# phi(k) of batch 2 issued earlier, k.v of later batches beside mm2 and by 64x64 corners, the z diagonal ahead of phi(q): one change to a linear-attention plus SwiGLU kernel

## The chip, the cores and the metric

The kernel runs on one core of a Trainium2 chip. The metric is the device time of one execution in microseconds; medians of several executions are quoted. The granted TensorE clock of each execution is recorded too.

The engines are called as in the profile: PE (TensorE, matmuls), PEld (its weight loads), DVE (VectorE), ACT (ScalarE), POOL (GpSimd), SP (the DMA queue used for outputs and transposes).

## The reference, cut to what matters

Linear attention over 8 batches (8 heads, 576 tokens, head dimension 64), then a SwiGLU block with 512 inputs, 1536 hidden, 512 outputs, on all 4608 tokens:

```python
q_p, k_p = phi(q), phi(k)                     # phi(x) = elu(x) + 1
kv  = einsum('bhsd,bhse->bhde', k_p, v)       # 64x64 per head
z   = sum(k_p, axis=2)
num = einsum('bhsd,bhde->bhse', q_p, kv)
den = einsum('bhsd,bhd->bhs', q_p, z)[..., None] + 1e-6
x   = (num / den) as (4608, 512)
out = (silu(x @ w_gate) * (x @ w_val)) @ w_out
```

## The kernel before: the parts that the change and the argument touch

The tokens go through the block in nine groups of 512. Each group is L1 (12 blocks of 4 + 4 matmuls 128x512, for gate and value) and then L2 (4 blocks of 12 matmuls). The attention of later batches is woven in: while group g is in L1 and L2, batch g+1 (`b1`) is prepared and mm2 makes the next `xT`, and exp and phi of batch g+2 (`b2`) run in L2. Lists of closures per slot say what is issued behind which block.

Names used below: `pG`, `pV` and `pX` are PSUM banks, which hold results of matmuls; to evict a bank is to copy its result out, so that it can be written again. `osb` holds results of L2 on their way out, `xT` is the input of L1, `R` the copy of k.v that mm2 multiplies by, `zd` the diagonal matrix from which one matmul ("the z matmul") makes z for the denominators, and s3 the steps that divide q by them. In the views `64*128` is the part of the array that a matmul uses (rows * columns), and `64x129` is the operand that streams through it, here 129 columns (N=129). An excursion is a stretch of matmuls in 64-row tiles between matmuls on the whole array.

```python
    def mm1(b, lp):                                  # k.v; lp = pair of heads
        if lp == 0:
            kvb[b] = (bank(), bank()) if b > 1 else ...
        W = 2 * D + (b > 1)                          # 129: v of two heads and a column of ones
        for j in range(J):                           # J = 9
            for (t, term_) in enumerate(terms_k(b, lp)):
                for hh in range(2):                  # rows 0..63 and 64..127 of the array
                    ...
                    nc.tensor.matmul(
                        out=kvb[b][hh][:, 256 * lp:256 * lp + W], lhsT=term_[rows, j, P * lp:P * lp + P], rhs=vv, ...)

    def zdiag(b, lp):                                # DVE: diagonal of z from the column of ones
        for hh in range(2):
            nc.vector.tensor_scalar(out=zd[:, 2 * hh + lp, :], in0=id16[:, :],
                                    scalar1=kvb[b][hh][:, 256 * lp + D:256 * lp + D + 1], ...)

    def steady(b, late=0):                           # what is woven into L1, by slot
        sl = [[] for _ in range(late)] + at(FB, [
            (0, lambda: phi_q(b, 0)), (1, lambda: phi_q(b, 1)), (1, lambda: mm1(b, 0)), (1, lambda: mm1(b, 1)),
            (2, lambda: zdiag(b, 0)), (2, lambda: zdiag(b, 1)), (2, lambda: r_copies(b)),
            (3 + (late > 0), lambda: zb(b)), ...     # zb: one matmul, ones x zd
    ...
    def first():                                     # woven into L1 and L2 of group 0
        ...
            (3, lambda: den1(0)), (4, lambda: num1(0)), (5, lambda: den1(1)), (6, lambda: num1(1)),
            (7, lambda: den2()), (7, lambda: exp_k(2, 0)), (7, lambda: exp_k(2, 1)), (8, lambda: num2()),
            (8, lambda: phi_k(2, 0)), (9, lambda: phi_k(2, 1)), (10, lambda: exp_q(2, 0)), (11, lambda: exp_q(2, 1))])
    ...
        for t in range(4):                           # L2 of group g
            if t == 3 and b1 < NG:
                mm2(b1, pV[2], "AVAV")               # 64x64 corners: num of the next group
            ...
            l2(g, t)
            ...
            l2_out(g, t, A if t == 1 else V)         # evict pso to osb, store
```

Of a product k.v over two heads (128 x 128) only the two 64x64 blocks on the diagonal are used; the old form computes all four.

## Time and profile before

| | before |
|---|---|
| median of 4 runs | 329.74 us (328.22 to 331.26) |
| profiled execution, span | 327.7 us |
| PE busy | 317.2 us (97%) |
| DVE, ACT busy | 216.2, 167.8 us (66%, 51%) |
| one 128x512 matmul, from start to the next start | 216 ns |

The busy time of PE is not its work: matmul records overlap (a 128x512 matmul is recorded with 380 ns, yet the next one starts after 216 ns). So I count by the start times in the timeline.

The page's first two parts, its busy times and the two lines of PE (busy tenths per slice; granted clock per slice in tenths):

```profile
PE 317.2 (97%) x1975; PEld 150.1 (46%) x1975; DVE 216.2 (66%) x400; ACT 167.8 (51%) x239; POOL 31.5 (10%) x47
PE   8999996899999999999999999999999999999994
PEclk9999999799999999999999999999999999999999
```

One dent, at 55 to 62 us: first idle, then a lower clock. The waits view of PE (who waited for whom: us in total, times, longest):

```profile
PE pG L280 <- DVE osb L311: 3.7, 1, 3.7
...
```

The windows view around it (busy us of each engine, then the granted clock, the DMA share, GB/s):

```profile
54.60:58.40 3.80, 0.12 (x1) 0.00 (x0) 3.77 (x8) 3.78 (x4) 0.10 (x1) 0.99 1.21 207
58.40:61.80 3.40, 3.37 (x9) 1.16 (x9) 1.17 (x2) 1.99 (x3) 0.64 (x1) 0.51 1.19 240
```

PE stands still for 3.8 us and then works 3.4 us at clock 0.51. What DVE does meanwhile is in its timeline (start, us, line, operation, count, idle before and who ended it):

```profile
53.42 0.46 DVE L125 TENSOR_SCALAR ek<-ek 128x1152 f16<-128x1152 f16 x1 [0.17 <-ACT ek L121]
53.91 1.43 DVE L127 SCALAR_TENSOR_TENSOR kp<-k,ek 128x576 f16<-128x576 f16 x2
55.26 0.68 DVE L311 TENSOR_SCALAR osb<-pV 128x512 f32<-128x512 f32 x1
55.86 0.45 DVE L125 TENSOR_SCALAR ek<-ek 128x1152 f16<-128x1152 f16 x1
56.34 1.43 DVE L127 SCALAR_TENSOR_TENSOR kp<-k,ek 128x576 f16<-128x576 f16 x2
57.69 0.68 DVE L311 TENSOR_SCALAR osb<-pG 128x512 f32<-128x512 f32 x1
```

The bank `pG` that L1 of group 1 needs first is evicted at 57.69, behind both halves of phi(k) of batch 2.

In the later groups k.v stands inside L1. The timeline of PE in group 2:

```profile
95.72 1.03 PE L280 MATMUL pV<-xT,wv 128*128 128x512 f16 x4
96.68 1.20 PE L170 MATMUL pX<-vm,kp 64*128 64x129 f16 x36
97.81 1.04 PE L280 MATMUL pG<-xT,wg 128*128 128x512 f16 x4
...
100.41 1.03 PE L280 MATMUL pV<-xT,wv 128*128 128x512 f16 x4
101.44 0.38 PE L200 MATMUL pX<-zd,ones 128*128 128x512 f16 x1
```

Four L1 matmuls take 0.863 us, so k.v could have started at 96.58: 0.10 us are lost in front of it. It holds PE from 96.68 to 97.81, 1.13 us.

### The profile page before, as it was taken

The page shows a single profiled execution, that of the slowest core. Times are in us where ns is not written, and L with a number is a line of the kernel's source. Part 1 is how long each engine was busy: PE and PEld are TensorE (multiplying, and loading weights), DVE is VectorE, ACT ScalarE, POOL GpSimd, SP SyncE. Part 2 cuts the span into 40 slices and gives each one's busy share as a digit, 9 for nine tenths or more (in the row PEclk, how much of TensorE's full clock was granted, in tenths as well). Part 3 has the DMA queues.
Part 4 walks back from the last instruction along what each step waited for, and adds up shares of the span by engine and source line. Part 5 has one row for each costly group of instructions (what it writes and reads, how often), then busy time and mean ns, then how long its engine had stood idle before and what let it go on. Part 6 is the DMA issues. An engine that isn't in the chain of part 4 may idle for free.

```text
span 327.7 us, 5115 instructions
## 1 busy us (share of the span) xinstructions
PE 317.2 (97%) x1975; PEld 150.1 (46%) x1975; DVE 216.2 (66%) x400; ACT 167.8 (51%) x239; POOL 31.5 (10%) x47
## 2 busy tenths in 40 slices
PE   8999996899999999999999999999999999999994
PEld 6644452344444444444444445444444444444443
DVE  3757747489978886889588858885887344234321
ACT  2869969536744584468446844584431233123310
POOL 8545300010001000100010000000000000000000
PEclk9999999799999999999999999999999999999999
DMA  7999999958386448553846440134012410140014
GB/s 102 195 200 200 205 207 208 249 98 157 79 169 92 79 89 162 78 92 80 169 65 107 67 112 0 26 71 95 14 24 50 98 30 2 33 92 4 2 32 96
DMA packets 40984, 32.18 MB, mean 98 GB/s; under 512 B 16256, under 2 KB 36480, under 8 KB 40960
## 3 DMA queue, kind: packets, MB, share of 16 engines
q0 software_dynamic: 20640, 18.88, 37.1%
q1 hardware_dynamic: 20160, 12.85, 17.7%
q8 instruction: 15, 0.25, 0.3%
q10 hardware_dynamic: 160, 0.13, 0.2%
q14 instruction: 9, 0.07, 0.1%
HBM read 37.75 MB, written 9.44 MB: 144 GB/s over the span
## 4 chain that ended last, share of the span: by engine, by line
PE 90%; DVE 4%; DMA 3%; ACT 1%; issue 1%; POOL 1%; SPq 0%; POOLq 0%; DVEq 0%; ACTq 0%
PE pV L280 27%; PE pG L280 27%; PE pV L301 14%; PE pG L301 13%; PE pX L280 2%; DMA q<-in_q_dram 2%; PE pX L170 2%; PE pX L252 2%; DVE kp L127 1%; DVE qp L127 1%; DMA out_dram<-osb 1%; PE pX L200 1%; DVE osb L311 1%; DVE hT L286 0%; ACT eq L367 0%
## 5 line engine op out<-in xcount | busy, mean ns | idle before, releaser
L280 PE MATMUL pG<-xT,wg 128*128 128x512 f16 x408 | 105.9, 382 | 3.7 <-DVE osb L311 3.7
L280 PE MATMUL pV<-xT,wv 128*128 128x512 f16 x420 | 108.9, 381 | 0.0
L285 ACT ACTIVATE sil<-pG 128x512 f16<-128x512 f32 x102 | 60.6, 598 | 92.6 <-PE pG L280 83.7
L286 DVE SCALAR_TENSOR_TENSOR hT<-pV,sil 128x512 f16<-128x512 f32 x105 | 72.2, 690 | 52.6 <-PE pV L280 40.0
L280 PEld LDWEIGHTS <-wg 128*128 128x128 f16 x432 | 41.5, 98 | 54.9 <-issue 6.8
L280 PEld LDWEIGHTS <-wv 128*128 128x128 f16 x432 | 42.4, 98 | 51.8 <-issue 1.1
L301 PEld LDWEIGHTS <-hT 128*128 128x128 f16 x420 | 39.8, 98 | 48.4 <-issue 2.0
L301 PE MATMUL pV<-wo,hT 128*128 128x512 f16 x216 | 50.2, 379 | 0.0
L301 PE MATMUL pG<-wo,hT 128*128 128x512 f16 x204 | 47.6, 380 | 0.0
L311 DVE TENSOR_SCALAR osb<-pV 128x512 f32<-128x512 f32 x18 | 12.4, 689 | 22.9 <-PE pV L301 22.9
L127 DVE SCALAR_TENSOR_TENSOR kp<-k,ek 128x576 f16<-128x576 f16 x24 | 17.1, 755 | 0.4
L127 DVE SCALAR_TENSOR_TENSOR qp<-q,eq 128x576 f16<-128x576 f16 x24 | 17.1, 755 | 0.4
L233 DVE TENSOR_TENSOR qp<-qp,rden 128x768 f16<-128x768 f16 x18 | 17.1, 951 | 0.2
L220 DVE TENSOR_REDUCE den<-prod 128x12 f32<-128x768 f16 x18 | 17.0, 942 | 0.0
L267 ACT ACTIVATE xT<-pX 128x512 f16<-128x512 f32 (+1 forms) x14 | 7.4, 579 | 16.7 <-PE pX L252 9.3
L121 ACT ACTIVATE ek<-k 128x1152 f16<-128x1152 f16 x14 | 15.5, 1154 | 0.1
L121 ACT ACTIVATE eq<-q 128x1152 f16<-128x1152 f16 x14 | 15.4, 1148 | 0.0
L147 ACT ACTIVATE vm<-v 128x1152 f16<-128x1152 f16 x12 | 14.1, 1172 | 0.0
L309 ACT ACTIVATE osb<-pG 128x512 f32<-128x512 f32 x8 | 4.7, 583 | 16.3 <-PE pG L301 16.3
L96 POOL DMA_DIRECT2D k<-in_k_dram x7 | 5.2, 742 | 76.4 <-DVE kp L127 54.9
L311 DVE TENSOR_SCALAR osb<-pG 128x512 f32<-128x512 f32 x9 | 6.2, 689 | 9.4 <-PE pG L301 9.4
L363 PE MATMUL pX<-sil,ones 128*128 128x256 f16 x51 | 8.9, 349 | 1.3 <-DVE sil L354 1.3
(97 smaller groups left out, 225.1 us busy)
## 6 DMA issues: line engine op xcount, KB each, us to landing
out_dram<-osb SPq DMA_DIRECT2D x70, 128.0 KB, 2.4
k<-in_k_dram POOLq DMA_DIRECT2D x7, 576.0 KB, 11.6
q<-in_q_dram POOLq DMA_DIRECT2D x7, 576.0 KB, 6.1
v<-in_v_dram POOLq DMA_DIRECT2D x7, 576.0 KB, 8.7
wg<-in_moe_w_gate_dram POOLq DMA_DIRECT2D x6, 256.0 KB, 12.1
wv<-in_moe_w_val_dram POOLq DMA_DIRECT2D x6, 256.0 KB, 12.0
wo<-in_moe_w_out_dram POOLq DMA_DIRECT2D x3, 512.0 KB, 15.8
k<-in_k_dram POOLq DMA_DIRECT2D x2, 288.0 KB, 5.9
```

Source lines behind the costliest of these rows:

```text
L121: nc.scalar.activation(out=e[:, s, :], in_=src[b % 2][:, s, :], func=AF.Exp, bias=0.0, scale=1.0)
L127: nc.vector.scalar_tensor_tensor(out=dst[b % 2][:, :, D * l:D * l + D], in0=src[b % 2][:, l, :].rearrange("p (j d) -> p j d", d=D), scalar ...
L147: nc.scalar.activation(out=vm[b % 2][:, :, s, 0:D].rearrange("p j l d -> p l j d"), in_=v16[b % 2][:, s, :].rearrange("p l (j d) -> p l j ...
L220: nc.vector.tensor_reduce(out=den[:, HL * j0:HL * j1], in_=prod[:, 0:j1 - j0, :].rearrange("p j (l d) -> p (j l) d", d=D), axis=AX.X, op=A ...
L233: nc.vector.tensor_tensor(out=qv, in0=qv, in1=rden[:, HL * j0:HL * j1].unsqueeze(2).to_broadcast([P, HL * (j1 - j0), D]), op=ALU.mult)
L267: nc.scalar.activation(out=dst, in_=ps[i][:, c00:], func=AF.Copy, bias=0.0, scale=1.0 / SC)
L280: nc.tensor.matmul(out=ps[:, :], lhsT=src[:, i, P * fb:P * fb + P], rhs=xT[i][g % 2][:, :], start=(i == 0), stop=(i == 3))
L285: nc.scalar.activation(out=s[:, :], in_=pg[:, :], func=AF.Silu, bias=0.0, scale=1.0)
L286: nc.vector.scalar_tensor_tensor(out=hT[g % 2][:, fb, :], in0=pv[:, :], scalar=SC, in1=s[:, :], op0=ALU.mult, op1=ALU.mult)
L301: nc.tensor.matmul(out=pso[(g, t)][:, :], lhsT=hT[g % 2][:, fb, P * t:P * t + P], rhs=wo[:, fb, :], start=(fb == 0), stop=(fb == FB - 1))
L311: nc.vector.tensor_scalar(out=o[:, :], in0=ps[:, :], scalar1=1.0 / SC, scalar2=None, op0=ALU.mult)
L363: nc.tensor.matmul(out=dst[:, 0:256], lhsT=ones[:, :], rhs=sil[0][:, 0:256], start=True, stop=True)
```

## The change

Its intent: at the boundary of groups 0 and 1, do phi(k) of batch 2 earlier so that the evictions are not behind it; move k.v of batches 3 to 7 next to mm2 in L2, where the array is in 64-row tiles anyway, using two banks that L2 has finished with; build the z diagonal before phi(q) on DVE; compute only the two useful 64x64 blocks of k.v.

```diff
 def mm1(b, lp):
-            kvb[b] = (bank(), bank()) if b > 1 else ((pV[2], pX[0]), (pX[2], pV[2]))[b]
+            kvb[b] = ((pV[2], pX[0]), (pX[2], pV[2]), (pX[0], pX[1]), (pV[0], pG[0]))[min(b, 3)]
...                                                  # batches 0 and 1 stay as they were; else:
+                    for e in range(2):
+                        nc.tensor.matmul(
+                            out=kvb[b][hh][D * e:D * e + D, 256 * lp:256 * lp + D + 1],
+                            lhsT=term_[rows, j, P * lp + D * e:P * lp + D * e + D],
+                            rhs=vm[b % 2][rows, j, 2 * lp + e, :], start=(j == 0), stop=(j == J - 1))
...
 def first():
-            (3, den1(0)), (4, num1(0)), (5, den1(1)), (6, num1(1)),
-            (7, den2()), (7, exp_k(2, 0)), (7, exp_k(2, 1)), (8, num2()),
-            (8, phi_k(2, 0)), (9, phi_k(2, 1)), (10, exp_q(2, 0)), (11, exp_q(2, 1))])
+            (3, den1(0)), (4, num1(0)), (4, exp_k(2, 0)), (5, den1(1)),
+            (5, phi_k(2, 0)), (6, num1(1)), (6, exp_k(2, 1)), (7, den2()),
+            (9, phi_k(2, 1)), (10, num2()), (10, exp_q(2, 0)), (11, exp_q(2, 1))])
...
+    def joint(b):                                   # k.v, z diagonal, R copies
+        for lp in range(2): mm1(b, lp)
+        for lp in range(2): zdiag(b, lp)
+        r_copies(b)
...
 def steady(b):                                       # batch 2: vcast, phi_q, joint in slots 0 to 3 of L1, z in slot 5
-            (0, phi_q(b, 0)), (1, phi_q(b, 1)), (1, mm1(b, 0)), (1, mm1(b, 1)), (2, zdiag ...), (2, r_copies(b)), (3, zb(b)) ...
+            (0, phi_q(b, 1)), (2, zb(b)) ...         # batches 3 on
 def prep(b):
+                      (3, preload of the silu table), (3, phi_q(b, 0))
...
             if t == 3 and b1 < NG:
                 mm2(b1, pV[2], "AVAV")
+                if b2 < B:
+                    joint(b2)
...
-            l2_out(g, t, A if t == 1 else V)
+            l2_out(g, t, A if t in (1, 3) else V)
```

(Lambdas are left out in the diff. The cast of v of batch 2 moved from the boundary into L1 of group 1, and in L2 what is left of s3 is now issued ahead of exp and phi of the batch after.)

More of the change, by code (lines that the diff above doesn't have):

```diff
@@ L67 @@
     epst = sb.tile([P, 1], FP32, name="epst")
-    R = two([P, 4, P + 1], FP16, "R")
+    R = two([P, 4, P], FP16, "R")
     qT = two([P, J, 2, P], FP16, "qT")
@@ L159, in mm1 @@
         if lp == 0:
-            kvb[b] = (bank(), bank()) if b > 1 else ((pV[2], pX[0]), (pX[2], pV[2]))[b]
-        W = 2 * D + (b > 1)
+            kvb[b] = ((pV[2], pX[0]), (pX[2], pV[2]), (pX[0], pX[1]), (pV[0], pG[0]))[min(b, 3)]
         for j in range(J):
@@ L166, in mm1 @@
                     if b < 2:
-                        vv = v16[b][rows, 2 * lp:2 * lp + 2, D * j:D * j + D]
-                    else:
-                        vv = vm[b % 2][rows, j, :, :].rearrange("p l c -> p (l c)")[:, 130 * lp:130 * lp + W]
-                    nc.tensor.matmul(
-                        out=kvb[b][hh][:, 256 * lp:256 * lp + W], lhsT=term_[rows, j, P * lp:P * lp + P], rhs=vv,
-                        start=(j == 0 and t == 0), stop=(j == J - 1 and t == len(terms_k(b, lp)) - 1))
+                        nc.tensor.matmul(
+                            out=kvb[b][hh][:, 256 * lp:256 * lp + P], lhsT=term_[rows, j, P * lp:P * lp + P],
+                            rhs=v16[b][rows, 2 * lp:2 * lp + 2, D * j:D * j + D],
+                            start=(j == 0 and t == 0), stop=(j == J - 1 and t == len(terms_k(b, lp)) - 1))
+                        continue
+                    for e in range(2):
+                        nc.tensor.matmul(
+                            out=kvb[b][hh][D * e:D * e + D, 256 * lp:256 * lp + D + 1],
+                            lhsT=term_[rows, j, P * lp + D * e:P * lp + D * e + D],
+                            rhs=vm[b % 2][rows, j, 2 * lp + e, :], start=(j == 0), stop=(j == J - 1))
     def zdiag(b, lp):
@@ L180, in r_copies @@
     def r_copies(b):
-        W = 2 * D + (b > 1)
+        W = D
         for hh in range(2):
@@ L188, in kv @@
     def kv(b):
-        c1 = D + (b > 1)
+        c1 = D if b < 2 else 0
         return lambda i, e: R[b % 2][D * e:D * e + D, i, c1 * e:c1 * e + D]
@@ L569, in first @@
             (2, lambda: t1(pX[0], 7, 9, A)), (2, lambda: mm1(1, 0)), (2, lambda: mm1(1, 1)), (2, lambda: r1_copies()),
-            (3, lambda: den1(0)), (4, lambda: num1(0)), (5, lambda: den1(1)), (6, lambda: num1(1)),
-            (7, lambda: den2()), (7, lambda: exp_k(2, 0)), (7, lambda: exp_k(2, 1)), (8, lambda: num2()),
-            (8, lambda: phi_k(2, 0)), (9, lambda: phi_k(2, 1)), (10, lambda: exp_q(2, 0)), (11, lambda: exp_q(2, 1))])
+            (3, lambda: den1(0)), (4, lambda: num1(0)), (4, lambda: exp_k(2, 0)), (5, lambda: den1(1)),
@@ L573, in first @@
+            (5, lambda: phi_k(2, 0)), (6, lambda: num1(1)), (6, lambda: exp_k(2, 1)), (7, lambda: den2()),
+            (9, lambda: phi_k(2, 1)), (10, lambda: num2()), (10, lambda: exp_q(2, 0)), (11, lambda: exp_q(2, 1))])
         return sl, w
-    def steady(b, late=0):
-        sl = [[] for _ in range(late)] + at(FB, [
-            (0, lambda: phi_q(b, 0)), (1, lambda: phi_q(b, 1)), (1, lambda: mm1(b, 0)), (1, lambda: mm1(b, 1)),
-            (2, lambda: zdiag(b, 0)), (2, lambda: zdiag(b, 1)), (2, lambda: r_copies(b)),
-            (3 + (late > 0), lambda: zb(b)), (3 + (late > 0), lambda: zb_copy(b)), (3 + (late > 0), lambda: s3_prod(b, 0)),
-            (4, lambda: s3_reduce(b, 0)), (5, lambda: s3_recip(b, 0)), (5, lambda: s3_prod(b, 1)),
-            (6, lambda: s3_scale(b, 0)), (7, lambda: s3_reduce(b, 1)), (7, lambda: tr(b, 0)),
-            (8, lambda: s3_recip(b, 1)), (8, lambda: s3_prod(b, 2)), (9, lambda: s3_scale(b, 1)),
-            (10, lambda: s3_reduce(b, 2)), (10, lambda: tr(b, 1)), (11, lambda: s3_recip(b, 2))])
-        w = at(4, [(0, f) for f in sum(sl[FB:], [])] + [(0, lambda: s3_scale(b, 2)), (0, lambda: tr(b, 2))])
-        if b == 2:
-            sl[0] += [lambda: vcast(2, 1)]
-        return sl[:FB], w
@@ new lines, in joint, with steady @@
+    def joint(b):
+        for lp in range(2):
+            mm1(b, lp)
+        for lp in range(2):
+            zdiag(b, lp)
+        r_copies(b)
+    def steady(b):
+        n = 5 if b == 2 else 2
+        items = [(n, lambda: zb(b)), (n, lambda: zb_copy(b)), (n, lambda: s3_prod(b, 0)),
+                 (n + 1, lambda: s3_reduce(b, 0)), (n + 2, lambda: s3_recip(b, 0)), (n + 2, lambda: s3_prod(b, 1)),
+                 (n + 3, lambda: s3_scale(b, 0)), (n + 4, lambda: s3_reduce(b, 1)), (n + 4, lambda: tr(b, 0)),
+                 (n + 5, lambda: s3_recip(b, 1)), (n + 5, lambda: s3_prod(b, 2)), (n + 6, lambda: s3_scale(b, 1)),
+                 (n + 7, lambda: s3_reduce(b, 2)), (n + 7, lambda: tr(b, 1)), (n + 8, lambda: s3_recip(b, 2)),
+                 (n + 9, lambda: s3_scale(b, 2)), (n + 9, lambda: tr(b, 2))]
+        if b == 2:
+            items = [(0, lambda: vcast(2, 0)), (1, lambda: vcast(2, 1)), (1, lambda: phi_q(2, 0)),
+                     (2, lambda: phi_q(2, 1)), (3, lambda: joint(2))] + items
+        else:
+            items = [(0, lambda: phi_q(b, 1))] + items
+        return at(FB, [x for x in items if x[0] < FB]), at(4, [(0, f) for (i, f) in items if i >= FB])
@@ L590, in prep @@
     def prep(b):
         return at(4, [(0, lambda: exp_k(b, 0)), (0, lambda: exp_k(b, 1)), (1, lambda: exp_q(b, 0)),
-                      (1, lambda: exp_q(b, 1)), (1, lambda: phi_k(b, 0)), (2, lambda: phi_k(b, 1))])
+                      (1, lambda: exp_q(b, 1)), (1, lambda: phi_k(b, 0)), (2, lambda: phi_k(b, 1)),
+                      (3, lambda: nc.scalar.preload_act_table_set("silu_and_others")), (3, lambda: phi_q(b, 0))])
     def ld_b(b):
@@ L640 @@
                 l2_out(0, t, V)
-    vcast(2, 0)
     nc.scalar.preload_act_table_set("silu_and_others")
@@ L648 @@
         if b1 < B:
-            sl, w = steady(b1, 2 if g == 1 else 0)
+            sl, w = steady(b1)
         if b2 < B:
@@ L668 @@
             l2(g, t)
-            for f in pre[t]:
+            for f in w[t] + pre[t]:
                 f()
-            for f in w[t]:
-                f()
-            l2_out(g, t, A if t == 1 else V)
+            l2_out(g, t, A if t in (1, 3) else V)
 _INS = ['q', 'k', 'v', 'moe_w_gate', 'moe_w_val', 'moe_w_out']
```

## The prediction

> **What bounds it now.** TensorE. The page has PE busy 317.2 of 327.7 us, but matmul records overlap, so I count from start to start in the timeline: 128x512 matmuls follow each other every 216 ns. The waits view shows one large wait of PE: 3.7 us at 54.7 us, L1 of group 1 on the DVE eviction of `osb`. After it the windows view gives half clock (0.51) from 58.4 to 61.8 us; the next 32 matmuls take 8.62 us instead of 6.91. The Trainium skill, "TensorE: Matmul & The Clock Gate" (the HAM clock gate), says that an idle window of about 3.4 us halves the clock; this trace agrees. The boundary costs 5.6 us together.
>
> In each later group k.v (36 matmuls 64*128, N=129) takes 1.13 us inside L1, with 0.10 us lost before it and 0.13 to 0.32 us in the 16 L1 matmuls after it: about 1.4 us. mm2 (8 or 16 matmuls 64*64) takes 0.45 to 0.57 us in L2.
>
> **What the change does.**
> 1. Boundary of groups 0 and 1. DVE now does phi(k) of batch 2 where it waited for `rr` (2.7 us), and the `num2` products move behind the second eviction. Adding up trace durations (exp 1.15, ln 0.6, `rr` exp 0.95, phi(k) 1.9 per half, eviction 0.68, x products 0.6 us): exp(k) at 47.9 and 51.1, second phi(k) 52.9 to 54.8, eviction of `pG` done at 55.4 instead of 58.4. L2 ends at 54.6: an idle of 0.9 us is left, and 0.3 us before the second L1 block, too short to halve the clock. K of batch 2 lands at 46.95 us, in time. Saved: 2.7 us of wait, 1.7 us of clock, 4.4 together.
> 2. k.v of batches 3 to 7 beside mm2: one excursion to 64-row tiles fewer. The skill, "TensorEngine Tiling (Array Packing)", Key Properties, says a change of mode drains TensorE; the 0.10 us before k.v agrees. Corners make 72 matmuls of N=65 from 36 of 129. In mm2 a set of four 64*64 matmuls costs its N columns plus about 27 ns (80 ns at N=128, 187 at N=384). 18 sets of about 54 ns are 1.0 us: the corners themselves save little. Saved: 1.4 - 1.0 = 0.4 us, 2.1 in five groups. Batch 2 keeps its own excursion: nothing.
> 3. Banks `pV[0]` and `pG[0]`: DVE evicts `osb` and two `xT`, builds z (0.8 us), then ACT copies R (0.7 us). Added up, R is copied 3.4 us after mm2 starts; the next L1 starts 4.1 us after it. It fits by 0.6 us. phi(k) ends about 1.2 us before k.v.
> 4. phi(q) and s3 earlier: DVE only, off the critical path.
>
> **Time.** 4.4 + 2.1 = 6.5 us, nearly all critical: 2.0%. I take off 0.4 us for small new waits: 323.5 us, 8 in 10 between 321.3 and 326.5. Faster by over 2%: 0.42; within 2%: 0.56; slower: 0.02.
>
> **What would show it.** Right: the wait on `osb` is near 1 us and no slice is at half clock; k.v follows mm2 at once, 72 matmuls in 0.9 to 1.1 us; no wait of PE on R or zd. Wrong: a wait on `osb` over 2 us; k.v over 1.3 us; L1 waiting for R at each group's start.
>
> **What would make it wrong.** If small matmuls start no faster than about 25 ns each whatever their tile, k.v by corners takes 1.8 us and loses 0.4 us in each group. If DVE is later than added up, the L2 banks come free too late. If the clock still drops, 1.7 us stay.

## The result, and the profile after

After: 320.8 us median of 4 runs (320.79 to 320.97), before 329.74; ratio 0.973, 95% interval 0.9685 to 0.9775: faster, and below the low end of my range (321.3). A ratio here is the mean time of one kernel's runs over that of the other's of the same rounds, so not quite the ratio of the medians.

The same lines of the page:

```profile
PE 311.8 (98%) x2191; PEld 148.5 (47%) x2191; DVE 211.3 (66%) x393; ACT 171.3 (54%) x246; POOL 31.9 (10%) x47
PE   8999999999999999999999999999999999999994
PEclk9999999999999999999999999999999999999999
```

The dent is gone. The waits view and the windows view:

```profile
...
PE pG L282 <- DVE osb L313: 0.6, 1, 0.6
...
```

```profile
52.00:55.50 3.50, 3.01 (x21) 1.15 (x20) 3.47 (x7) 3.47 (x6) 0.04 (x1) 1.00 1.22 209
55.50:58.90 3.40, 3.21 (x15) 1.39 (x15) 2.71 (x8) 3.37 (x5) 0.70 (x1) 1.00 1.18 239
```

And DVE at the boundary:

```profile
49.82 1.43 DVE L127 SCALAR_TENSOR_TENSOR kp<-k,ek 128x576 f16<-128x576 f16 x2
...
52.42 0.68 DVE L313 TENSOR_SCALAR osb<-pV 128x512 f32<-128x512 f32 x1
53.02 0.45 DVE L125 TENSOR_SCALAR ek<-ek 128x1152 f16<-128x1152 f16 x1
53.50 1.43 DVE L127 SCALAR_TENSOR_TENSOR kp<-k,ek 128x576 f16<-128x576 f16 x2
54.85 0.68 DVE L313 TENSOR_SCALAR osb<-pG 128x512 f32<-128x512 f32 x1
```

`pG` is evicted at 55.53; I had added up 55.4. The boundary did what was predicted. The timeline of PE in the L2 of group 2, where mm2 and k.v now stand together (first and last lines):

```profile
117.95 0.35 PE L254 MATMUL pX<-qT,R 64*64 64x192 f16 x5
...
118.41 0.19 PE L172 MATMUL pV<-vm,kp 64*64 64x65 f16 x1
...
119.02 0.20 PE L172 MATMUL pG<-vm,kp 64*64 64x65 f16 x2
119.15 2.76 PE L303 MATMUL pG<-wo,hT 128*128 128x512 f16 x12
```

k.v holds PE from 118.41 to 119.15, 0.74 us, not the 1.0 that I had predicted. No wait of PE on R or `zd` appears in its waits view.

Where the 8.5 us of the profiled spans (327.7 to 319.2) went, by the start of the first matmul of each stage:

| stage | before, us | after, us | difference |
|---|---|---|---|
| start to L2 of group 0 | 38.83 | 39.09 | +0.26 |
| L2 of group 0, to the first L1 matmul of group 1 | 19.60 | 16.50 | -3.10 |
| first 32 L1 matmuls of group 1 (clock) | 8.62 | 7.26 | -1.36 |
| k.v of batch 2, in L1 of group 1 | 1.13 | 0.71 | -0.42 |
| rest of L1 of group 1 | 14.04 | 14.04 | 0.00 |
| L2 of group 1 (now with k.v of batch 3) | 10.92 | 11.56 | +0.64 |
| groups 2 to 6 | 166.89 | 162.41 | -4.48 |
| groups 7 and 8 | 67.66 | 67.64 | -0.02 |

The boundary gives 3.10 + 1.36 = 4.5 us (predicted 4.4). Batches 3 to 7 give 4.48 - 0.64 = 3.8 us (predicted 2.1), batch 2 gives 0.4 us (predicted nothing).

### The profile page after: what moved, and what is told of

Its sections match the earlier page's. It is cut to its first block, busy times and chain, and to the rows that moved or that the text cites. A ratio compares the mean times of both kernels' runs of the same rounds, so it can differ in the third digit from the quotient of the medians.

```text
span 319.2 us, 5573 instructions
## 1 busy us (share of the span) xinstructions
PE 311.8 (98%) x2191; PEld 148.5 (47%) x2191; DVE 211.3 (66%) x393; ACT 171.3 (54%) x246; POOL 31.9 (10%) x47
## 4 chain that ended last, share of the span: by engine, by line
PE 89%; DMA 4%; DVE 2%; POOL 2%; ACT 2%; issue 1%; SPq 0%; POOLq 0%; ACTq 0%
PE pV L282 28%; PE pG L282 27%; PE pV L303 14%; PE pG L303 13%; DMA wv<-in_moe_w_val_dram 3%; PE pX L282 2%; PE pX L254 1%; DVE osb L313 1%; DMA out_dram<-osb 1%; PE pV L172 1%; DVE xT L435 1%; ACT rr L432 1%; ACT rr L429 1%; POOL k L99 0%; POOL v L99 0%
## 5 line engine op out<-in xcount | busy, mean ns | idle before, releaser
L311 ACT ACTIVATE osb<-pG 128x512 f32<-128x512 f32 x15 | 8.8, 589 | 19.9 <-PE pG L303 19.8
L217 DVE TENSOR_TENSOR prod<-qp,zbc 128x768 f16<-128x768 f16 x18 | 9.3, 516 | 1.4 <-ACT zbc L208 1.3
```

Source lines behind the costliest of these rows:

```text
L217: nc.vector.tensor_tensor(out=prod[:, 0:j1 - j0, :], in0=qp[b % 2][:, j0:j1, :], in1=zbc[:, :].unsqueeze(1).to_broadcast([P, j1 - j0, HL * ...
```

## The experiments

Three parts were changed together: the boundary, the place of k.v (with the DVE order around it), and the corners. My miss lies in the last two. The theories: A, a set of four corners takes its columns plus a few ns, wherever it stands; B, corners are as dear as I had predicted (54 ns per set) and the place beside mm2 did the rest; later C, the rate at which matmuls start sets the time of a set, not its columns.

### The kernel before with corners alone

```diff
 mm1, batches 2 to 7: one matmul 64*128 of 129 columns
-> two matmuls 64*64 of 65 columns (as in the change), at the old place in L1; R copies and kv() to match
```

> The kernel before with k.v of batches 2 to 7 by 64x64 corners, at its old place inside L1; nothing else. Theory A (corners are cheap wherever they stand: weights of one set load behind the columns of the set before, 33 ns per set of four at N=65): k.v takes 0.71 to 0.75 us instead of 1.13, six times 0.4 us, so about 327.3 us against 329.7 (ratio 0.993), gap and half clock at the boundary as before. Rival B (my prediction: 54 ns per set; corners gain only where they stand directly behind mm2): k.v 1.0 to 1.1 us here, ratio 0.998 to 1.0.

Measured: 329.25 us, ratio 0.9988 (0.995 to 1.0027), same. By the time alone B would seem right. The trace says otherwise; group 2, PE and then DVE:

```profile
96.37 0.78 PE L172 MATMUL pX<-vm,kp 64*64 64x65 f16 x72
97.08 1.04 PE L282 MATMUL pG<-xT,wg 128*128 128x512 f16 x4
...
99.68 1.03 PE L282 MATMUL pV<-xT,wv 128*128 128x512 f16 x4
101.14 0.38 PE L202 MATMUL pX<-zd,ones 128*128 128x512 f16 x1 [0.43 <-DVE zd L179]
```

```profile
97.86 0.45 DVE L125 TENSOR_SCALAR eq<-eq 128x1152 f16<-128x1152 f16 x1
98.35 1.43 DVE L127 SCALAR_TENSOR_TENSOR qp<-q,eq 128x576 f16<-128x576 f16 x2
99.69 0.68 DVE L288 SCALAR_TENSOR_TENSOR hT<-pV,sil 128x512 f16<-128x512 f32 x1
100.29 0.80 DVE L179 TENSOR_SCALAR zd<-id,pX 128x128 f16<-128x128 f16 x4
```

The corners did take 0.71 us instead of 1.13, in all six batches. But the z matmul then waits for `zd`, which stands behind phi(q) in DVE's queue and comes no earlier. The 0.42 us are given back as a wait in five groups (the waits view sums it to 2.0 us); only batch 2 keeps its gain. Theory A is right on the cost, and my expectation from it was wrong on the time.

### The same, with the z diagonal ahead of phi(q)

```diff
-            (0, phi_q(b, 0)), (1, phi_q(b, 1)), (1, mm1(b, 0)), (1, mm1(b, 1)), (2, zdiag(b, 0)), (2, zdiag(b, 1)), (2, r_copies(b)),
+            (0, mm1(b, 0)), (0, mm1(b, 1)), (1, zdiag(b, 0)), (1, zdiag(b, 1)), (1, r_copies(b)), (1, phi_q(b, 0)), (2, phi_q(b, 1)),
```

> The kernel before with corners at the old place in L1, and the z diagonal put ahead of phi(q) on VectorE with k.v one slot earlier. In the run with corners alone the z matmul waited 0.4 us for zd in five groups and ate the gain. If the order on VectorE is the cause: no wait on zd, 2.0 us (and the 0.17 us per group that the kernel before lost there) less than that run: about 326.8 us against 329.3. If the wait has another cause: still 329 us.

Measured: 326.57 us, ratio 0.9899 (0.9853 to 0.9946); no wait of PE on `zd` is left. DVE in group 2:

```profile
97.10 0.75 DVE L179 TENSOR_SCALAR zd<-id,pX 128x128 f16<-128x128 f16 x4
97.76 0.45 DVE L125 TENSOR_SCALAR eq<-eq 128x1152 f16<-128x1152 f16 x1
98.25 1.43 DVE L127 SCALAR_TENSOR_TENSOR qp<-q,eq 128x576 f16<-128x576 f16 x2
```

The times hold the clock of the boundary too: two of the four executions had a granted clock of 1.00 (325.80 and 325.97 us), two had less (327.16 and 328.02). Against the executions of the kernel before at the same clock in these rounds they are on average 2.5 to 3.1 us faster.

The order on DVE was the cause of the wait. This run also put k.v one slot earlier, but the run with k.v back in L1 below tells the two apart: there k.v and the z matmul stand where they stand with corners alone, only phi(q) is done earlier, and no wait on `zd` is left either. Corners make PE earlier, the order lets it use that. The order without corners was not run; from the trace of before it could give no more than the 0.12 to 0.31 us a group that the z matmul was late there.

### The change with the old form of k.v at the new place

```diff
 the kernel after, but mm1 of batches 2 to 7 as before: 36 matmuls 64*128, N=129
```

> The kernel after, with k.v of batches 2 to 7 in the old form (36 matmuls 64*128, N=129), at its new place. Theory A: k.v takes 1.0 to 1.15 us instead of 0.74, six times 0.3 to 0.4 us, so about 322.9 us (ratio to before 0.979). Rival B (the place alone did it): as after, 320.8 us (0.973).

Measured: 323.62 us, ratio 0.9816 (0.9773 to 0.986); k.v takes 1.13 us beside mm2 as it did in L1. Corners are worth 2.8 us of the change (323.62 to 320.8), not the little that I had predicted. Rival B falls. It is 0.7 us slower than theory A expected; most of that is mm2's exit, which k.v in 64*128 tiles does not save (in group 2 mm2 holds PE for 0.56 us here and 0.46 in the kernel after; 0.10 us in each of five groups).

### The change with k.v back in L1

```diff
-        n = 5 if b == 2 else 2
+        n = 5 if b == 2 else 3
-            items = [(0, phi_q(b, 1))] + items
+            items = [(0, phi_q(b, 1)), (1, mm1(b, 0)), (1, mm1(b, 1)), (2, zdiag(b, 0)), (2, zdiag(b, 1)), (2, r_copies(b))] + items
-                if b2 < B:
-                    joint(b2)
 and k.v of batches 3 to 7 in two banks of pX again
```

> The kernel after, with k.v, z diagonal and R copies of batches 3 to 7 put back into L1 (k.v in slot 1, z matmul in slot 3), corners and the early phi(q) of the first half kept. Value of the place alone: its own drain and mode change cost 0.10 us before and 0.10 us after k.v in five groups, 1.0 us: 321.8 us (ratio to before 0.976). If the z matmul then waits for zd as in the run with corners alone (0.4 us five times): up to 323.8 us.

Measured: 321.67 us, ratio 0.9748 (0.9705 to 0.9792), no wait on `zd`. The place itself is worth 0.18 us a group by the traces (table below), 0.8 to 0.9 us in all; the first theory of the expectation holds. (This run and the kernel after were timed in different rounds, so the traces are the better measure.)

The runs line up when only group 2 is measured, from its first L1 matmul to that of group 3, which the boundary does not touch:

| kernel | group 2, us |
|---|---|
| before | 33.36 |
| corners alone | 33.37 |
| corners, z diagonal first | 32.78 |
| after, k.v back in L1 | 32.78 |
| after, old form of k.v | 33.09 |
| after | 32.60 |

Groups 3 to 5 agree with this within 0.05 us, but for one: with corners and z diagonal first they take 32.87 us, because k.v takes 0.80 us there instead of 0.71 (not followed further).

### How long a set of four corners takes

I had taken 27 ns per set on top of the columns. Two looks, each with the same 72 matmuls per batch and other widths:

```diff
-   out=kvb[b][hh][D * e:D * e + D, 256 * lp:256 * lp + D + 1],      rhs=vm[b % 2][rows, j, 2 * lp + e, :]
+   out=kvb[b][hh][D * e:D * e + D, 256 * lp + 32:256 * lp + D + 1], rhs=vm[b % 2][rows, j, 2 * lp + e, 32:]     # N=33
+   out=kvb[b][hh][D * e:D * e + D, 256 * lp:256 * lp + 2 * D + 1],  rhs=both heads of vm, 129 columns           # N=129
```

> The kernel after, corners of k.v with 33 columns (values 32 to 63 and the ones) instead of 65; wrong results on purpose, same number of instructions. Theory A (a set of four takes its columns, N/2.4 ns, plus about 6 ns): 20 ns per set, k.v beside mm2 0.50 us instead of 0.74. Rival C (matmuls of this kind start about 8 ns apart whatever N is; the start times in the trace are 8.3 ns apart in the second half): stays at 0.72 to 0.75 us.

> The kernel after, corners of k.v with 129 columns instead of 65 (each corner multiplies both heads of the pair, as the old form did), correct results, same number of instructions, twice the columns. Theory A: 60 ns per set, k.v 1.15 to 1.25 us, so by itself as slow as the old form (1.13 us). Rival C: between, columns and starts overlap: 54 ns per set, 1.05 to 1.15 us. If my prediction's 27 ns per set were right at all: 81 ns, 1.5 us or more.

One execution each: 321.01 us for N=33 (wrong results) and 323.42 us for N=129 (correct). The timelines of PE at k.v of batch 2, N=33 and then N=129:

```profile
62.98 0.75 PE L172 MATMUL pX<-vm,kp 64*64 64x33 f16 x72
63.66 1.04 PE L282 MATMUL pG<-xT,wg 128*128 128x512 f16 x4
```

```profile
62.95 1.22 PE L172 MATMUL pX<-vm,kp 64*64 64x129 f16 x72
64.10 1.04 PE L282 MATMUL pG<-xT,wg 128*128 128x512 f16 x4
```

To the next L1 matmul that is 0.69 us at N=33, 0.71 at N=65 (in the kernel after) and 1.15 at N=129. From the start times inside k.v beside mm2, a set of four takes 33 to 34 ns at N=33, the same at N=65, and 57 ns at N=129 (means within each half of the 18 sets; between the halves two sets take 50 and 53 ns at N=33 and at N=65, which stays unexplained). Halving the columns from 65 shortens k.v by only 0.02 to 0.03 us, so theory A's form (columns plus 6 ns) falls and C holds: about 8.3 ns from one matmul to the next is the limit below some 80 columns (an estimate: 33 ns x 2.4 columns per ns, from 216 ns for 512), the columns above it. What sets the 8.3 ns stays open: every one of these matmuls also loads its own weights, and no run separates the start of a matmul from the load or from the supply of instructions. At N=129 the corners take as long as the 36 old matmuls (1.13 us beside mm2 for both). So the gain inside k.v is in the columns that are no longer computed, 129 to 65, as far as that limit allows; more and smaller tiles for the same columns save nothing there, only mm2's exit (group 2 takes 32.99 us with corners of N=129 and 33.09 with the old form).

### The boundary alone, and the clock alone

```diff
 the kernel before with the new slots of first(), and vcast(2, 0), vcast(2, 1) in slots 0 and 1 of L1 of group 1
```

> The kernel before with only the reordered work at the boundary of groups 0 and 1 (exp and phi of k of batch 2 between the den and num steps, num2 later, cast of v into L1). If the boundary is worth what I predicted: wait on osb about 0.8 us instead of 3.7, no half clock, 4.4 us less, about 325.3 us (ratio 0.9865). If part of that was given back in L1 of group 1 (DVE late there): 2 to 3 us less, with the first matmuls of L1 over 216 ns apart.

Measured: 325.33 us, ratio 0.987 (0.9834 to 0.9907). The waits view of PE:

```profile
...
PE pG L280 <- DVE osb L311: 0.6, 1, 0.6
...
```

The profiled span is 4.5 us shorter (327.7 to 323.2), as predicted, and no half clock comes before the last 2.2 us; the medians differ by 4.9 us. That the time itself was met to 0.03 us is luck: the kernel before was 0.5 us slower in these rounds than in the first. The first 32 L1 matmuls of group 1 take 7.26 us here, 0.35 more than at 216 ns each (the prediction had 0.3 us there); behind them nothing was given back.

```diff
+    warm(30, pX[0])            # dummy matmuls, 256 columns, results unused
     for g in range(1, NG):
```

> The kernel before with 30 dummy matmuls of 256 columns (about 3.2 us, results unused) put on TensorE where it idles 3.7 us before group 1; the wait on osb itself stays. If the half clock comes from that idle: the next 32 matmuls take 6.9 us instead of 8.6, 1.7 us less in the profile, about 328.0 us (ratio 0.995), and the scatter of before's times (3 us) shrinks to a few tenths. If the half clock has another cause: it stays, ratio 1.0.

Measured: 328.72 us, ratio 0.997 (0.9931 to 1.0008): by the time alone, not told from before. The windows view of this run, behind the gap:

```profile
59.40:66.40 7.00, 6.98 (x32) 3.03 (x31) 4.04 (x7) 3.98 (x6) 0.64 (x1) 1.00 1.17 255
```

L1 still starts 3.9 us after L2 ends, yet its first 32 matmuls take 7.00 us at full clock instead of 8.62 at half. The idle is the cause of the half clock. (The scatter of this run is 0.9 us, not the few tenths that were expected.) Why the median gains only about 1.5 us (330.21 in these rounds): before does not lose the clock every time. Of its seven executions here, the two with a granted clock of 1.00 took 328.28 and 328.66 us, the two at 0.987 took 330.88 and 331.51, three at 0.991 to 0.992 lie between. The four with the gap filled lie at 0.996 to 1.00 and within 328.27 to 329.16 us; no execution of the kernel after is below 0.996 (in its profiled one the half clock comes only in the last 1.3 us, when the work is over). So most of the scatter of before is the clock.

That the same idle does not always cost the clock can be seen in a trace. The run with corners and z diagonal first has the boundary of before, and PE stands still for 3.7 us; its windows view in the gap and behind it shows full clock:

```profile
55.60:59.20 3.60, 0.00 (x0) 0.00 (x0) 3.57 (x7) 3.58 (x4) 0.04 (x1) 1.00 1.21 207
59.30:66.20 6.90, 6.90 (x101) 3.37 (x101) 3.20 (x5) 3.34 (x5) 0.60 (x1) 1.00 1.17 256
```

### Can it be beaten?

0.6 us of waiting at the boundary and 0.35 us in the first L1 blocks are left in the kernel after. Two versions were run next to it; on that chip the kernel after was timed again:

> The kernel after again, on the chip of the next two runs, to compare them with: 320.8 us, ratio to before 0.973.

Measured: 321.13 us, ratio 0.9746 (0.9724 to 0.9768).

```diff
-            (9, phi_k(2, 1)), (10, num2()) ...
+            (10, num2()) ...
                 l2_out(0, t, V)
+    phi_k(2, 1)                 # behind the four evictions of group 0
```

> The kernel after, with phi(k) of the second half of batch 2 behind the four evictions of group 0 instead of ahead of the second one. L1 of group 1 waits 0.75 us for the eviction of pG and 0.35 us more inside its first 32 matmuls; with the eviction directly behind L2's second block both waits go: 1.0 us less, 319.8 us. If DVE is then late in L1 of group 1 (phi(k), two phi(q), z), the gain comes back as waits there: 320.8 us.

Measured: 320.23 us, ratio 0.9718 (0.9694 to 0.9742). L1 of group 1 starts without a wait and its first 32 matmuls take 7.00 us. Some comes back: the z matmul of batch 2 starts 0.13 us late and the L1 matmul behind it another 0.27 us late. DVE, which now does phi(k) here, is the likely reason; the trace was not followed further.

```diff
+ as the run before, and mm1 of batches 0 and 1 by corners of 64 columns
```

> As the run before, and k.v of batches 0 and 1 by corners as well (54 matmul pairs in the start, 18 in L2 of group 0, N=64). Where TensorE is the limit a pair of N=128 takes 55 ns and a set of four N=64 about 33: batch 1 gains 0.4 us; batch 0 at most 1.2 us if TensorE is the limit there, nothing if it waits for loads and DVE. 318.8 to 319.5 us.

Measured: 321.07 us, ratio 0.9744 (0.9718 to 0.977), and a wider scatter (319.93 to 322.5): a miss. Batch 1 did go from 1.11 to 0.71 us. But in the start, PE stops for 1.8 us in the middle of batch 0's corners, with no releaser in the trace:

```profile
16.03 0.20 PE L166 MATMUL pV<-v,kp 64*64 64x64 f16 x2
18.00 0.22 PE L166 MATMUL pX<-v,kp 64*64 64x64 f16 x2 [1.76 <-issue]
```

"Issue" means that the profile shows nothing that it waited for. A transfer of 16 KB on the queue called "instruction" lies at 15.5 to 16.5 us in that trace, while the loads keep the DMA engines full, so a late supply of instructions is a guess; it was not tested. (The kernel after has such a transfer at 15.2 to 16.2 us without a stop, so the transfer alone is not enough.)

```diff
+ phi_k(2, 1) behind the evictions; k.v of batch 1 alone by corners; zb(2), zb_copy(2), s3_prod(2, 0) one slot later
```

> The kernel after with three edits: phi(k) of the second half of batch 2 behind the evictions (as in the run before: 320.2 us), k.v of batch 1 by corners (0.71 instead of 1.11 us in the run with all corners), and the z matmul of batch 2 one slot later, where it waited 0.3 us for zd after the first edit. Sum: 0.4 us for batch 1, 0.3 to 0.4 us for z of batch 2, so about 319.5 us. If DVE in L1 of group 1 is simply full, the z wait reappears further on and 319.9 us remain.

Measured: 319.85 us (319.65 to 320.45, 6 runs), ratio 0.9699 (0.9666 to 0.9732), the fastest of all, but short of 319.5. The z matmul no longer waits; instead PE waits once for ACT:

```profile
65.89 1.02 PE L284 MATMUL pG<-xT,wg 128*128 128x512 f16 x4 [0.64 <-ACT sil L289]
```

So the rival of that expectation holds in substance: in L1 of group 1 the wait moved from z to a gate bank. Against the kernel after it is a gain of about 0.4% across two sets of rounds, small beside the scatter of before; the two were not run in the same rounds.

## Why the prediction was right or wrong

- **Boundary, 4.4 us: right.** 4.5 us by the stages, 4.5 by the spans and 4.9 us by the medians of the boundary alone. The sum of trace durations put the eviction at 55.4 us, it was 55.53 us; the wait on `osb` was 0.6 us (predicted "near 1"); no half clock. What I had not seen is that the clock's 1.7 us are lost in most executions of before, not in all.
- **"In mm2 a set of four 64*64 matmuls costs its N columns plus about 27 ns", and from it "18 sets of about 54 ns are 1.0 us: the corners themselves save little": this step failed.** A set takes 33 ns at N=65, k.v 0.71 to 0.74 us. The 27 ns were real, but only in the first set of an excursion. I had read them off excursions of two sets (80 ns at N=128, 187 at N=384), where the only interval between sets follows the first set. The trace of before held the answer: in the excursion of four sets at 123.3 us, the intervals are 107, 82 and 136 ns at N=192, 192 and 320, that is 80, 80 and 133 ns of columns with 27, 2 and 3 ns on top:

```profile
123.33 0.35 PE L252 MATMUL pX<-qT,R 64*64 64x192 f16 x5
123.44 0.24 PE L252 MATMUL pV<-qT,R 64*64 64x192 f16 x1
...
123.52 0.43 PE L252 MATMUL pX<-qT,R 64*64 64x320 f16 x5
123.66 0.30 PE L252 MATMUL pV<-qT,R 64*64 64x320 f16 x1
...
```

  (A line of x5 is one whole set and the first matmul of the next.) k.v by corners shows the same: its first set takes 52 ns where it opens the excursion, in L1, and 29 ns behind mm2.
- **"Batch 2 keeps its own excursion: nothing": wrong by the same step.** It gained 0.42 us from the corners, at no change of place.
- **"One excursion fewer" for batches 3 to 7: right in kind.** Predicted 2.1 us for place and corners together, measured 3.8. Per group: k.v went from 1.13 to 0.74 us, mm2 gave up its 0.10 us of exit to it, the 0.10 us in front of k.v and on average 0.18 us of waiting for `zd` went too: 0.39 + 0.10 + 0.10 + 0.18 = 0.77 us, and five times that is the 3.8. With k.v back in L1, 3.0 of the 3.8 us are kept, so most of the gain is corners and order, not the place.
- **I put the 0.13 to 0.32 us behind k.v down to L1 matmuls and had no cause for them.** The matmul that was late was z's, waiting for `zd`. So item 4, "phi(q) and s3 earlier: DVE only, off the critical path", was wrong too: the order of the z diagonal and phi(q) decides whether the corners' gain arrives at all (33.37 against 32.78 us in group 2).
- **Banks: right.** R is copied 3.0 us after mm2 starts in group 3, L1 follows at 3.8 us, no wait on R; phi(k) ends 1.2 us before k.v, as predicted.
- **The 0.4 us taken off for small new waits did not come.**

Together: 1.7 us more in batches 3 to 7, 0.4 us in batch 2 and 0.4 us not lost are 2.5 us, and 323.5 - 2.5 = 321.0, against 320.8 measured. The mechanism at the boundary was right. Beside it the cost of a set was mis-sized (54 ns predicted, 33 measured), and the wait of the z matmul was not recognised.

The opposite danger, that small matmuls start too slowly for corners to pay, did not come: with four tiles in turn they start every 8.3 ns on average.

## What to carry to other kernels

Read a cost per item from a run long enough to separate the first item from the rest; two items give a price that contains the entry. When a step on the critical engine gets shorter, look at what the next step waits for: here the whole gain of the corners turned into a wait until another engine's order was changed. A short idle of TensorE in front of dense work can cost half as much again in clock (here 1.7 us behind an idle of 3.7), and not in every execution, so it shows as scatter as well as time.

## What the Trainium skill lacked or had wrong

- "TensorE: Matmul & The Clock Gate", Part 1, "Wait — 56ns, not 53.3ns?": it says that start to start never drops below about 25 ns, however few the columns. With the four 64x64 tiles used in turn, a set of four starts every 33 to 34 ns at N=33 and at N=65, 8.3 ns per matmul, each with new weights. Part 3 of the page has the distance of the starts within one pack of tiles, but not the time from one set to the next when the same tiles are used again and again.
- "TensorEngine Tiling (Array Packing)", Instruction Overhead: it says that a matmul of one column takes as long as one of 60. In kind this agrees (0.73 us for 72 matmuls at N=33, 0.74 at N=65), but for four tiles the limit lies near 33 ns per set (at N=129 it is 57). What column tiling costs by turning off fast weight load (which its Restrictions name), the page does not say: here only the first set of an excursion shows 27 ns on top of its columns, and later sets 2 to 3 ns, so the load of the next weights seems to be hidden behind the current set.
- The same page, Key Properties: a change of tiling mode drains TensorE, without a figure. Here it is about 0.10 us on the way in and 0.10 us on the way out. k.v in 64*64 tiles behind mm2 saved mm2's exit (0.46 instead of 0.56 us); k.v in 64*128 tiles behind it did not (0.56 us).
- "TensorE: Matmul & The Clock Gate", Part 1: an idle window of about 3.4 us halves the clock, and the windows run freely. It does not say how often an idle little longer than a window costs the clock. Here, by the granted clock, an idle of 3.7 us cost it in five of seven executions of the kernel before (0.987 to 0.992), and filled with dummy matmuls in none of four.
